# Loading w of the first four chunks in two-token runs of 320 bytes, with running sums by pair member

## The chip, the cores and the metric

The kernel runs on one core of a Trainium2 chip. The core has a matrix engine (PE, with its weight loads shown as PEld), a vector engine (DVE), an activation engine (ACT), a general engine (POOL), a queue engine (SP) and 16 DMA engines that move data between the chip's memory (HBM) and the on-chip buffers. Each engine takes its instructions in order. The metric is the device time of one execution in microseconds (us).

## The reference

A recurrent attention over 768 tokens, for 4 batches of 8 heads of 40 features each (`r`, `k`, `v`, `w`, `a`, `b`, each 4 x 8 x 768 x 40, float32), and then a feed-forward layer on the result:

```python
for t in range(S):
    y[:, :, t] = np.einsum('bhd,bhde->bhe', rt, state)
    Sa = np.einsum('bhde,bhe->bhd', state, at)
    state_decay = state * wt[:, :, None, :] - np.einsum('bhd,bhe->bhde', Sa, bt)
    state = state_decay + np.einsum('bhd,bhe->bhde', vt, kt)
...
h = x @ w_in
g = np.maximum(h, 0.0) ** 2
return g @ w_out
```

Here `x` is `y` laid out as 3072 tokens of 320 features; `w_in` is 320 x 2048, `w_out` 2048 x 320. `w` decays the state at each token, so over a stretch of tokens it enters as a product, which the kernel forms as the exponential of a running sum of logarithms.

## The kernel before

The tokens are cut into 12 chunks of 64. Tokens of a chunk lie on partitions: 64 for the batches 0 and 1 (g = 0) and 64 for the batches 2 and 3 (g = 1). A batch of such a group is called here a member, and each member has 8 heads. So `raw_w`, 128 x 16 x 40 numbers, has on partition 64g + t the 16 heads of group g at token t.

For each chunk c the kernel does this with w:

- `ldw c` loads it (`load`, `go_w`), in two transfers of 160 KB, each with runs of 40 numbers, 160 bytes. For chunk 0 there are four transfers of 80 KB, by group and member: member 0 (`ldw 0 h0`) on SP, member 1 (`ldw 0 h1`) on ACT.
- `ln c` (ACT, L598) takes the logarithm into `lnW`; `hi c` and `lo c` split it into two bf16 parts (`hi` a cast, `lo` the rest). For chunk 0 each is done in two halves, by member.
- `ci c` and `cf c` (PE, recorded at L388) form the running sums over the chunk's tokens by multiplying with a triangle of ones. `ci` puts tokens on partitions (320 columns a matmul), `cf` puts features on partitions and tokens on columns. For chunks 0 to 3 `ci` uses the 128 x 128 matrix `UTB`, two triangles of 64 on the diagonal, so one matmul covers both groups. `cf` of chunks 0, 1 and 2 uses `UTB` too (`wide_sums`); `cf` of chunk 3 and of all later chunks works in pairs of 64-row matmuls with `UTI`, one for each group.
- `ec`, `eg` and `ef` (ACT, L624, L562, L674) are exponentials of the sums, into `Gin`, `iG` and `GT`. `eg` of chunk 0 is done in two halves.
- `tb`, `tk` (DVE, L580) and `tA` (DVE, L712) multiply turned k, b and a with `iG` and `GT`; what follows are the triangles `EN` and `CX` (DVE, L737), the state `S`, `s` (L838), and the feed-forward matmuls (L958 and L388).

For chunks 0 to 3 (`BY8`) k, b, a and r are loaded in runs of eight tokens, 1280 bytes, and turned by PE; v is loaded in 160-byte runs in all chunks. From chunk 4 on k and b are loaded in 160-byte runs too.

The order of the work on each engine is written out by hand in `ORDER`, and the program issues exactly that order. The loads on SP begin: `ldw 0 h0`, `ldb 0`, `ldk 0`, `lda 0`, `ldw 1`, `ldv 0`, `ldb 1`, `ldr 0`, `ldw 2`, `lda 2`, `ldv 1`, `ldw 3`, `ldb 2`, `ldk 2`, `ldv 2`, `ldr 1`. On PE `TR 0` (r of chunk 0 turned) stands ahead of `NU 0`, `TA 1` and `TU 1`.

The constants (`UTI`, `UTB`, `IDQ`, `IDb`, `MSK`, `MSKI`) are made at the start by POOL's `affine_select`, 14 instructions of 64 x 64 (L266); the casts of w of chunk 0 on POOL stand behind them.

## Time and profile before

| | |
|---|---|
| time, three runs | 237.29, 237.42, 239.2 us; median 237.42 |
| the profiled execution, its own time | 238.79 us |
| its span, from the first to the last instruction | 237.1 us |
| mean granted TensorE clock | 0.998 |
| packets of all DMA queues | 121689 of 38.78 MB, 105770 of them under 512 bytes |
| transfers of w on SP | 22 of 160 KB and 2 of 80 KB; 2 more of 80 KB on ACT |

A page of the profile shows the busy time of each engine, the chain of work that ended last (followed back from the last instruction, at each step to what released it), groups of instructions by line, and the DMA queues. Other views show the chain in order of time, the instructions of an engine in order of time, and the busy time in given stretches. Times count from the start of the span. A DMA that SP issues shows as SPq with the time that the issue took; the transfer lands later. In brackets stands how long an engine was idle before an instruction, and what released it. "x2" merges two instructions that follow one another.

### The profile page before, as it was taken

To read this page: it belongs to the slowest core of one execution; us is meant where nothing else is said; L and a number is where in the kernel's file an instruction comes from. 1 tells how busy PE (TensorE), PEld (TensorE's weight loads), DVE (VectorE), ACT (ScalarE), POOL (GpSimd) and SP (SyncE) were. 2 spreads that over 40 slices of the span, in tenths; PEclk is the share of its full clock that TensorE was granted. 3 is DMA by queue.
4 is the path that set the end of the run, shared out by engine and by line. 5 is a ranking of instruction groups with operands and counts; after the bars stand their busy time and mean duration, and the time that the engine had idled before them with its cause. 6 is when DMAs were issued, how large, how long until landed. Compare 5 with 4: busy or idle time off the path is not lost.

```text
span 237.1 us, 11681 instructions
## 1 busy us (share of the span) xinstructions
PE 217.9 (92%) x5249; PEld 167.7 (71%) x5249; DVE 181.0 (76%) x236; ACT 175.0 (74%) x233; POOL 130.9 (55%) x138
## 2 busy tenths in 40 slices
PE   7587887889999999999998999999987999999993
PEld 2366776668787777777776778777775777877771
DVE  7468999697989877888977989799877687756220
ACT  3637957848997996897997989996767984652911
POOL 8552729056696547579394944907986620730600
PEclk9999999999999999999999999999999999999999
DMA  5998879998898998999999889989998995931104
GB/s 122 209 228 154 176 160 260 271 210 203 269 179 165 174 191 155 157 187 156 181 166 188 173 151 170 177 179 184 177 155 165 186 159 124 194 13 30 30 3 110
DMA packets 121689, 38.78 MB, mean 164 GB/s; under 512 B 105770, under 2 KB 121638, under 8 KB 121638
## 3 DMA queue, kind: packets, MB, share of 16 engines
q1 hardware_dynamic: 119862, 37.04, 82.4%
q10 hardware_dynamic: 1776, 0.98, 1.6%
q8 instruction: 41, 0.67, 1.2%
q14 instruction: 10, 0.08, 0.1%
HBM read 28.84 MB, written 3.93 MB: 138 GB/s over the span
## 4 chain that ended last, share of the span: by engine, by line
PE 74%; DMA 7%; SPq 7%; ACT 3%; issue 3%; DVE 2%; POOL 2%; ACTq 0%; POOLq 0%; DVEq 0%
PE pb L388 43%; PE pb L958 23%; PE pb L392 5%; PE pb L396 3%; DMA KBT<-KB 3%; DMA raw_r<-in_r_dram 2%; DMA raw_kb<-in_b_dram 2%; SPq L445 2%; SPq L430 2%; SPq L454 2%; ACT VU L374 1%; DVE STb L838 1%; ACT GT L674 1%; SPq L432 1%; POOL lo L382 1%
## 5 line engine op out<-in xcount | busy, mean ns | idle before, releaser
L994 POOL TENSOR_TENSOR G<-G 128x1024 bf16<-128x1024 bf16 x22 | 41.6, 1896 | 35.9 <-ACT G L986 33.8
L388 PE MATMUL pb<-WOUT,G 128*128 128x320 bf16 x384 | 56.9, 300 | 0.0
L958 PE MATMUL pb<-XT,WIN 128*128 128x256 bf16 x384 | 48.7, 273 | 1.1 <-ACT VU L374 1.0
L986 ACT ACTIVATE G<-pb 128x1024 bf16<-128x1024 f32 x39 | 39.3, 1021 | 12.1 <-PE pb L958 10.2
L388 PEld LDWEIGHTS <-G 128*128 128x128 bf16 x384 | 35.6, 98 | 14.1 <-issue 0.2
L958 PEld LDWEIGHTS <-WIN 128*128 128x128 bf16 x384 | 34.8, 98 | 8.5 <-issue 2.4
L737 DVE TENSOR_TENSOR CX<-pb,MSKI 128x1024 bf16<-128x1024 f32 x24 | 28.9, 1221 | 5.8 <-PE pb L388 5.6
L737 DVE TENSOR_TENSOR EN<-pb,MSK 128x1024 bf16<-128x1024 f32 x24 | 29.0, 1217 | 4.3 <-PE pb L388 3.8
L382 POOL TENSOR_TENSOR KB<-raw_kb,iG 128x640 bf16<-128x640 f32 x12 | 18.4, 1543 | 5.5 <-DMA raw_a<-in_a_dram 2.9
L712 DVE TENSOR_TENSOR AR<-pb,GT 128x512 bf16<-128x512 bf16 x24 | 15.8, 685 | 4.6 <-PE pb L396 1.8
L838 DVE TENSOR_TENSOR STb<-pb,GT 40x640 bf16<-40x640 f32 x22 | 18.1, 821 | 0.6
L996 ACT ACTIVATE G<-G 128x1024 bf16<-128x1024 bf16 x17 | 17.8, 1053 | 0.2
L382 POOL TENSOR_TENSOR lo<-lnW,hi 128x640 bf16<-128x640 f32 (+1 forms) x10 | 13.5, 1352 | 7.4 <-ACT hi L374 6.2
L958 PE MATMUL pb<-XT,WLAST 64*128 64x256 bf16 x192 | 17.5, 272 | 0.0
L388 PEld LDWEIGHTS <-EN 64*64 64x64 bf16 (+1 forms) x768 | 14.6, 110 | 3.2 <-issue 2.5
L378 POOL CAST hi<-lnW 128x640 bf16<-128x640 f32 (+1 forms) x10 | 6.9, 692 | 16.7 <-ACT lnW L598 15.9
L374 ACT ACTIVATE osb<-pb 128x640 f32<-128x640 f32 (+1 forms) x10 | 6.5, 650 | 12.2 <-PE pb L388 12.1
L647 ACT ACTIVATE Gin<-pb 64x320 f32<-64x320 f32 x32 | 13.7, 429 | 2.0 <-PE pb L388 1.5
L920 DVE TENSOR_TENSOR Yb<-pb,Gin 128x640 bf16<-128x640 f32 (+1 forms) x24 | 12.4, 551 | 3.2 <-PE pb L388 3.1
L374 ACT ACTIVATE VU<-pb 64x640 bf16<-64x640 f32 x17 | 11.8, 696 | 3.8 <-PE pb L388 3.5
L374 ACT ACTIVATE AR<-pb 128x512 bf16<-128x512 bf16 x20 | 11.0, 596 | 4.7 <-PE pb L392 3.5
L988 DVE TENSOR_SCALAR G<-pb 128x1024 bf16<-128x1024 f32 x9 | 11.0, 1223 | 3.5 <-PE pb L958 3.3
(131 smaller groups left out, 442.8 us busy)
## 6 DMA issues: line engine op xcount, KB each, us to landing
raw_kb<-in_b_dram SPq DMA_DIRECT2D x24, 160.0 KB, 4.3
raw_v<-in_v_dram SPq DMA_DIRECT2D x24, 160.0 KB, 4.4
raw_kb<-in_k_dram SPq DMA_DIRECT2D x22, 160.0 KB, 5.0
raw_a<-in_a_dram SPq DMA_DIRECT2D x22, 160.0 KB, 4.9
raw_w<-in_w_dram SPq DMA_DIRECT2D x22, 160.0 KB, 4.4
raw_r<-in_r_dram SPq DMA_DIRECT2D x22, 160.0 KB, 4.1
out_dram<-osb SPq DMA_DIRECT2D x22, 160.0 KB, 2.6
G<-in_moe_w_in_dram SPq DMA_DIRECT2D x10, 256.0 KB, 5.8
```

Of the source, the lines that this page charges most:

```text
L374: alts.append(("ACT", c_act(n), lambda: nc.scalar.activation(out=o_(), in_=i_(), func=ACTF.Copy, scale=1.0 if scale is None else scale)))
L382: return [("POOL", 40 + 2.35 * n, lambda: nc.gpsimd.tensor_tensor(out=o_(), in0=a_(), in1=b_(), op=op)), ("DVE", c_dve(n), lambda: nc.vect ...
L388: return lambda: nc.tensor.matmul(out=o_(), lhsT=l_(), rhs=r_(), start=start, stop=stop, skip_group_check=True)
L647: nc.scalar.activation(out=Gin[c % NGI][rows(g), NP * jh:NP * jh + NP, :].rearrange("p j e -> p (j e)"), in_=slot(hb, FP32)[rows(g), g, 0: ...
L712: ew(f"tA {c} g{g}", [("DVE", c_dve(512), lambda g=g: nc.vector.tensor_tensor(out=steps(AR[q2][:, 0, g]), in0=turned(ha, g), in1=steps(GT[ ...
L737: ew(f"m{nm} {c} g{g}", [("DVE", c_dve(1024), lambda: nc.vector.tensor_tensor(out=dst[q2][:, g].rearrange("p q i t -> p (q i) t"), in0=slo ...
L838: ew(f"s {c} q{q}", [("DVE", c_dve(2 * n), lambda q=q: nc.vector.tensor_tensor(out=STb[q2][live(q), :, q, 0:D], in0=slot(hs, FP32)[live(q) ...
L920: return [("DVE", c_dve(2 * (f1 - f0)), lambda: nc.vector.tensor_tensor(out=Yb[q2][:, :, to:to + f1 - f0], in0=slot(hy, FP32)[:, :, f0:f1] ...
L958: return lambda: nc.tensor.matmul(out=o_(), lhsT=l_(), rhs=r_(), start=begins and opens(hf, x), stop=ends and not opens(hf, x), skip_group ...
L986: ("ACT", c_act(1024), lambda gb=gb, hf=hf: nc.scalar.activation(out=gb, in_=slot(hf, FP32)[:], func=ACTF.Relu)),
L994: ("POOL", 1900, lambda gv=gv: nc.gpsimd.tensor_tensor(out=gv, in0=gv, in1=gv, op=ALU.mult)),
L996: ("ACT", c_act(1024), lambda gv=gv: nc.scalar.activation(out=gv, in_=gv, func=ACTF.Square))],
```

## The change

For chunks 0 to 3 w is loaded with two consecutive tokens in one run of 80 numbers, 320 bytes. A pair of tokens now lies on one partition: partition 64x + 32g + p holds tokens 2p and 2p + 1 of member x of group g, with 8 heads of two tokens. That takes four transfers of 80 KB a chunk, by member and group. Chunk 0 has as many as before, two on SP and two on ACT; chunks 1, 2 and 3 have four on SP.

The logarithm writes `lnW` with the token of the pair (i) outermost, 8 heads each. A running sum is then over pairs and over the two members of a pair: for each member x of the batches (its 64 partitions), for each i, and for `hi` and `lo`, one 64-row matmul with the matrix `UT2[rows(x), i]`, 64 x 128, which puts the tokens of both groups into 128 columns. `ci` of a chunk becomes eight 64-row matmuls of 320 columns (chunk 0: two times eight of 160) for four of 128 rows; `cf` becomes 32 64-row matmuls of 128 columns, for 16 of 128 rows (chunks 0, 1, 2) or 32 64-row ones of 64 columns (chunk 3). The sums come out in the places that they had in chunks 0 to 2.

The halves of chunk 0 are now by heads (0 to 3, 4 to 7 of each member), so both halves of `ln 0` read all four transfers, and each half of `eg 0` is two instructions. `UTB` is gone; `UT2` is made by four `affine_select` of 64 x 128 from a mask that DVE writes into `EN` beforehand with three memsets, and `UTI` by two of 64 x 128 for four of 64 x 64. `ORDER` is as it was.

```diff
-    UTB = buf("UTB", [128, 128], BF16)[0]
...
+    UT2 = buf("UT2", [128, 2, 128], BF16)[0]
...
+    gate = EN[0][:].rearrange("p a b c d -> p (a b c d)")[:, 0:128]
+    nc.vector.memset(gate, 1.0)
+    for g in range(2):
+        nc.vector.memset(gate[64 * g:64 * g + 32, 64:128], 0.0)
+    for g in range(2):
+        for i in range(2):
+            nc.gpsimd.affine_select(out=UT2[rows(g), i, :], in_=gate[rows(g), :],
+                                    pattern=[[1, 128]], compare_op=ALU.is_ge, fill=0.0,
+                                    base=-i, channel_multiplier=-2)
...
+        nc.gpsimd.affine_select(out=UTI[rows(g), :].rearrange("p (x t) -> p x t", x=2),
+                                in_=ones[rows(g), :].rearrange("p (x t) -> p x t", x=2),
+                                pattern=[[0, 2], [1, 64]], compare_op=ALU.is_ge, fill=0.0,
+                                base=0, channel_multiplier=-1)
...
         def go_w(js, q_):
-            for g in range(2):
-                if len(js) == 2:
-                    q_.dma_start(out=raw_w[c % NW][rows(g)], in_=half(w, g))
-                else:
+            for x in js if c in BY8 else ():
+                for g in range(2):
+                    p0 = 64 * x + 32 * g
                     q_.dma_start(
-                        out=raw_w[c % NW][rows(g), NP * js[0]:NP * js[0] + NP, :],
-                        in_=w[2 * g + js[0], :, t0, :].rearrange("h t e -> t h e"))
+                        out=raw_w[c % NW][p0:p0 + 32].rearrange("p (h i) e -> p h (i e)", i=2),
+                        in_=w[2 * g + x, :, t0, :].rearrange("h (p i) e -> p h (i e)", i=2))
+            for g in range(0 if c in BY8 else 2):
+                q_.dma_start(out=raw_w[c % NW][rows(g)], in_=half(w, g))
...
-        return c == 0 or f"cf {c}" in WHOLE
...
-        if wide_sums(c):
+        if c in BY8:
             return flat(h, FP32).rearrange("p (m g t) -> p g m t", g=2, t=L)
...
+                for at in ([slice(4 * y + 2 * js[0], 4 * y + 2 * js[0] + 2) for y in range(2)]
+                           if len(js) == 1 else [slice(0, 8)]):
+                    nc.scalar.activation(out=o_[:, :, at], in_=i_[:, :, at], func=ACTF.Exp,
+                                         scale=-1.0)
...
-               reads=[("raw", "w", c % NW, jh) for jh in js] + [("act",)],
+               reads=[("raw", "w", c % NW, jh) for jh in range(2)] + [("act",)],
...
+                for x in (h_, l_):
+                    for i in range(2):
+                        for g in range(2):
+                            ms.append(mm(
+                                lambda g=g, a0=a0, a1=a1: slot(hd, FP32)[:, g, 0:n].rearrange(
+                                    "p (j e) -> p j e", e=D)[:, a0:a1],
+                                lambda g=g, i=i: UT2[rows(g), i, :],
+                                lambda x=x, g=g, i=i, a0=a0, a1=a1: x[
+                                    rows(g), 8 * i + a0:8 * i + a1, 0:D],
+                                x is h_ and i == 0 and a0 == 0, x is l_ and i == 1))
...
+            for p in range(2 * js[0], 2 * js[-1] + 2) if c in BY8 else ():
                 for x in (h_, l_):
-                    if wide_sums(c):
-                        ms.append(mm(
-                            lambda p=p: flat(hf, FP32)[:, 128 * p:128 * p + 128],
...
+                    for i in range(2):
+                        for g in range(2):
+                            ms.append(mm(
+                                lambda p=p, g=g: slot(hf, FP32)[:, g, 128 * p:128 * p + 128],
+                                lambda x=x, p=p, g=g, i=i: x[
+                                    rows(g), 8 * i + 2 * p:8 * i + 2 * p + 2, :].rearrange(
+                                        "p h e -> p (h e)"),
+                                lambda g=g, i=i: UT2[rows(g), i, :],
+                                x is h_ and i == 0 and p == 0, x is l_ and i == 1))
```

More of the change, by code (lines that the diff above doesn't have):

```diff
@@ L267, in tri_const @@
                                 base=0, channel_multiplier=-1)
-    UTB = buf("UTB", [128, 128], BF16)[0]
-    IDQ = buf("IDQ", [128, 128], BF16)[0]
-    nc.vector.memset(UTB[:], 0.0)
-    nc.vector.memset(IDQ[:], 0.0)
-    for g in range(2):
-        for x in range(2):
-            tri_const(UTI[rows(g), rows(x)], ones[rows(g), 0:64], ALU.is_ge)
-    for g in range(2):
-        tri_const(UTB[rows(g), rows(g)], ones[rows(g), 0:64], ALU.is_ge)
-    for g in range(2):
-        tri_const(IDQ[rows(g), rows(g)], ones[rows(g), 0:64], ALU.is_equal)
-    for g in range(2):
-        tri_const(IDb[rows(g), :], ones[rows(g), 0:64], ALU.is_equal)
-    for g in range(2):
-        tri_const(MSK[rows(g), :], ones[rows(g), 0:64], ALU.is_gt)
-    for g in range(2):
-        tri_const(MSKI[rows(g), :], ones[rows(g), 0:64], ALU.is_ge)
     NW, NKBR, NA, NR, NV = 2, 2, 2, 2, 2
@@ L322 @@
     WOUT = buf("WOUT", [128, NFB, DM], BF16)[0]
+    UT2 = buf("UT2", [128, 2, 128], BF16)[0]
+    IDQ = buf("IDQ", [128, 128], BF16)[0]
+    gate = EN[0][:].rearrange("p a b c d -> p (a b c d)")[:, 0:128]
[7 more added lines that the diff above has]
+                                    base=-i, channel_multiplier=-2)
+    nc.vector.memset(IDQ[:], 0.0)
+    for g in range(2):
[4 more added lines that the diff above has]
+    for g in range(2):
+        tri_const(IDQ[rows(g), rows(g)], ones[rows(g), 0:64], ALU.is_equal)
+    for g in range(2):
+        tri_const(IDb[rows(g), :], ones[rows(g), 0:64], ALU.is_equal)
+    for g in range(2):
+        tri_const(MSK[rows(g), :], ones[rows(g), 0:64], ALU.is_gt)
+    for g in range(2):
+        tri_const(MSKI[rows(g), :], ones[rows(g), 0:64], ALU.is_ge)
     for x in GT:
@@ L427, in go_w @@
         def go_w(js, q_):
-            for g in range(2):
-                if len(js) == 2:
-                    q_.dma_start(out=raw_w[c % NW][rows(g)], in_=half(w, g))
-                else:
+            for x in js if c in BY8 else ():
+                for g in range(2):
+                    p0 = 64 * x + 32 * g
                     q_.dma_start(
-                        out=raw_w[c % NW][rows(g), NP * js[0]:NP * js[0] + NP, :],
-                        in_=w[2 * g + js[0], :, t0, :].rearrange("h t e -> t h e"))
+                        out=raw_w[c % NW][p0:p0 + 32].rearrange("p (h i) e -> p h (i e)", i=2),
+                        in_=w[2 * g + x, :, t0, :].rearrange("h (p i) e -> p h (i e)", i=2))
+            for g in range(0 if c in BY8 else 2):
+                q_.dma_start(out=raw_w[c % NW][rows(g)], in_=half(w, g))
         for js in ((0,), (1,)) if c == 0 else ((0, 1),):
@@ L511, in flat @@
         return slot(h, dt)[:].rearrange("p b x -> p (b x)")
-    def wide_sums(c):
-        return c == 0 or f"cf {c}" in WHOLE
     def sums(c, h):
-        if wide_sums(c):
+        if c in BY8:
             return flat(h, FP32).rearrange("p (m g t) -> p g m t", g=2, t=L)
@@ L559, in keys_by8, with exps @@
         for js in ((0,), (1,)) if c == 0 else ((0, 1),):
-            at = slice(4 * js[0], 4 * js[-1] + 4)
-            ew(f"eg {c}" + f" h{js[0]}" * (2 - len(js)), [
-                ("ACT", c_act(512 * len(js)), lambda at=at: nc.scalar.activation(
-                    out=igt.rearrange("p (g m) t -> p g m t", g=2)[:, :, at],
-                    in_=sums(c, hf)[:, :, at], func=ACTF.Exp, scale=-1.0))],
+            def exps(js=js):
+                o_ = igt.rearrange("p (g m) t -> p g m t", g=2)
+                i_ = sums(c, hf)
+                for at in ([slice(4 * y + 2 * js[0], 4 * y + 2 * js[0] + 2) for y in range(2)]
+                           if len(js) == 1 else [slice(0, 8)]):
+                    nc.scalar.activation(out=o_[:, :, at], in_=i_[:, :, at], func=ACTF.Exp,
+                                         scale=-1.0)
+            ew(f"eg {c}" + f" h{js[0]}" * (2 - len(js)), [("ACT", c_act(512 * len(js)), exps)],
                reads=[hf + (jh,) for jh in js], writes=[("iG", jh) for jh in js], free=[hf])
@@ L596, in prep, with part, log @@
         for js in ((0,), (1,)) if c == 0 else ((0, 1),):
-            x, at, k_ = f" h{js[0]}" * (2 - len(js)), slice(NP * js[0], NP * js[-1] + NP), 320 * len(js)
-            ew(f"ln {c}{x}", [("ACT", c_act(k_), lambda at=at: nc.scalar.activation(
-                out=lw[:, at], in_=raw_w[c % NW][:, at], func=ACTF.Ln))],
-               reads=[("raw", "w", c % NW, jh) for jh in js] + [("act",)],
+            x, k_ = f" h{js[0]}" * (2 - len(js)), 320 * len(js)
+            def part(t, js=js):
+                if len(js) == 2:
+                    return t
+                return t.rearrange("p (i h) e -> p i h e", i=2)[:, :, 4 * js[0]:4 * js[0] + 4]
+            def log(js=js, part=part):
+                o_, i_ = lw[:], raw_w[c % NW][:]
+                if c in BY8:
+                    o_ = o_.rearrange("p (i h) e -> p i h e", i=2)
+                    i_ = i_.rearrange("p (h i) e -> p i h e", i=2)
+                    at = slice(4 * js[0], 4 * js[-1] + 4)
+                    o_, i_ = o_[:, :, at], i_[:, :, at]
+                nc.scalar.activation(out=o_, in_=i_, func=ACTF.Ln)
+            ew(f"ln {c}{x}", [("ACT", c_act(k_), log)],
+               reads=[("raw", "w", c % NW, jh) for jh in range(2)] + [("act",)],
                writes=[("lnW", jh) for jh in js])
-            ew(f"hi {c}{x}", copy_alts(lambda at=at: h_[:, at, 0:D], lambda at=at: lw[:, at], k_,
+            ew(f"hi {c}{x}", copy_alts(lambda part=part: part(h_[:, :, 0:D]),
+                                       lambda part=part: part(lw[:]), k_,
                                        True, engines=("POOL", "DVE", "ACT")),
                reads=[("lnW", jh) for jh in js], writes=[("hi", jh) for jh in js])
-            ew(f"lo {c}{x}", mul_alts(lambda at=at: l_[:, at, 0:D], lambda at=at: lw[:, at],
-                                      lambda at=at: h_[:, at, 0:D], k_, ALU.subtract),
+            ew(f"lo {c}{x}", mul_alts(lambda part=part: part(l_[:, :, 0:D]),
+                                      lambda part=part: part(lw[:]),
+                                      lambda part=part: part(h_[:, :, 0:D]), k_, ALU.subtract),
                reads=[("lnW", jh) for jh in js] + [("hi", jh) for jh in js],
@@ L613, in prep @@
                 ms = []
-                for jh in js:
-                    for x in (h_, l_):
-                        ms.append(mm(
-                            lambda jh=jh: slot(hd, FP32)[:, jh, 0:n].rearrange(
-                                "p (j e) -> p j e", e=D),
-                            lambda: UTB[:], lambda x=x, jh=jh: x[:, NP * jh:NP * jh + NP, 0:D],
-                            x is h_, x is l_))
-                pe(f"ci {c}" + f" h{js[0]}" * (2 - len(js)), "D", n, ms,
+                a0, a1 = 4 * js[0], 4 * js[-1] + 4
+                for x in (h_, l_):
+                    for i in range(2):
+                        for g in range(2):
+                            ms.append(mm(
[5 more added lines that the diff above has]
+                                x is h_ and i == 0 and a0 == 0, x is l_ and i == 1))
+                pe(f"ci {c}" + f" h{js[0]}" * (2 - len(js)), "R", 160 * len(js), ms,
                    reads=[(x, jh) for x in ("hi", "lo") for jh in js], writes=[hd],
@@ L654, in prep @@
             ms = []
-            for p in range(4 * js[0], 4 * js[-1] + 4):
+            for p in range(2 * js[0], 2 * js[-1] + 2) if c in BY8 else ():
                 for x in (h_, l_):
-                    if wide_sums(c):
-                        ms.append(mm(
-                            lambda p=p: flat(hf, FP32)[:, 128 * p:128 * p + 128],
-                            lambda x=x, p=p: x[:, 2 * p:2 * p + 2, :].rearrange(
-                                "p h e -> p (h e)"),
-                            lambda: UTB[:], x is h_ and p % 4 == 0, x is l_))
-                        continue
+                    for i in range(2):
+                        for g in range(2):
+                            ms.append(mm(
[5 more added lines that the diff above has]
+                                x is h_ and i == 0 and p == 0, x is l_ and i == 1))
+            for p in range(0 if c in BY8 else 8):
+                for x in (h_, l_):
                     for g in range(2):
@@ L670, in prep @@
             pe(f"cf {c}" + f" h{js[0]}" * (2 - len(js)),
-               *(("D", 128) if wide_sums(c) else ("R", L)), ms,
+               "R", 128 if c in BY8 else L, ms,
                reads=[(x, jh) for x in ("hi", "lo") for jh in js],
```

## The prediction

> **What bounds the kernel now.** I read the page first, then the windows, then the chain of waits in order of time, then the timelines of SP and DVE over the first 36 us. From the page:

> ```profile
> span 237.1 us, 11681 instructions
> PE 217.9 (92%) x5249; PEld 167.7 (71%) x5249; DVE 181.0 (76%) x236; ACT 175.0 (74%) x233; POOL 130.9 (55%) x138
> q1 hardware_dynamic: 119862, 37.04, 82.4%
> PE 74%; DMA 7%; SPq 7%; ACT 3%; issue 3%; DVE 2%; POOL 2%; ACTq 0%; POOLq 0%; DVEq 0%
> ```

> PE is busy 92% of the span and holds 74% of the chain. DMA and the SP queue hold 14%, and the question is where. The windows (length, then busy time and instructions of PE, PEld, DVE, ACT, POOL, clock, DMA share, GB/s) and four rows of the chain (start, duration, what) answer it:

> ```profile
> 0.00:20.00 20.00, 14.71 (x187) 9.21 (x187) 13.83 (x35) 9.87 (x14) 11.45 (x28) 1.00 0.89 180
> 20.00:36.00 16.00, 13.06 (x426) 11.26 (x423) 14.43 (x19) 12.80 (x16) 7.69 (x11) 1.00 0.78 170
> 60.00:100.00 40.00, 39.63 (x1000) 30.68 (x994) 32.93 (x40) 34.40 (x48) 25.45 (x25) 1.00 0.91 185
> ```

> ```profile
> 13.95 5.90 DMA raw_r<-in_r_dram
> ...
> 25.80 5.34 DMA raw_kb<-in_b_dram
> ...
> 39.23 0.76 PE pb L388 x40
> ...
> 45.63 1.05 PE pb L958 x8
> ```

> From 60 us on PE works 39.63 of 40 us: nothing about loads of w can speed that up, but a time won earlier passes through it to the end. In the first 36 us PE has 8.2 us of idle (36 less 14.71 and 13.06), and the chain goes through loads: r of chunk 0 lands 5.90 us after its issue, b of chunk 2 after 5.34. That is the only stage where the change acts, since it concerns w of chunks 0 to 3.

> **The SP queue.** SP issues nearly all loads in one fixed order. Its timeline (start, duration, transfers; nothing between them but a few tenths):

> ```profile
> 5.16 1.24 SPq L460 DMA_DIRECT2D raw_a<-in_a_dram  x2
> 6.44 1.60 SPq L430 DMA_DIRECT2D raw_w<-in_w_dram  x2
> 8.09 3.64 SPq L454 DMA_DIRECT2D raw_v<-in_v_dram  x2
> 14.67 1.36 SPq L430 DMA_DIRECT2D raw_w<-in_w_dram  x2
> 16.12 4.31 SPq L460 DMA_DIRECT2D raw_a<-in_a_dram  x2
> 21.91 3.02 SPq L430 DMA_DIRECT2D raw_w<-in_w_dram  x2
> 24.97 1.43 SPq L445 DMA_DIRECT2D raw_kb<-in_b_dram  x2
> ```

> An undisturbed pair takes 1.24 (a, 5.16) to 1.36 us (w, 14.67): 0.62 to 0.68 us an issue. Three pairs take much longer: v of chunk 0 by 2.4, a of chunk 2 by 3.07, w of chunk 3 by 1.66 us, 7.1 us together. Each stands behind, or is, a load in 160-byte runs. I read these as a queue that is full until packets ahead have been served.

> **Price of a packet.** Two windows of one microsecond, one while w of chunk 1 and v of chunk 0 (160-byte runs) are under way, one while b and r (1280-byte runs) are:

> ```profile
> 12.00:13.00 1.00, 1.00 (x12) 0.61 (x10) 0.43 (x1) 0.00 (x0) 0.00 (x0) 1.00 1.11 169
> 15.00:16.00 1.00, 0.37 (x5) 0.23 (x6) 1.00 (x2) 0.67 (x1) 1.00 (x1) 1.00 0.98 284
> ```

> At a share of one these are 169/1.11 = 152 and 284/0.98 = 290 GB/s, so with 16 engines a 160-byte packet takes 16 x 160/152 = 16.8 ns and a 1280-byte packet 70.6 ns. The line through both gives 24.5 ns for 320 bytes, which no row shows. The bounds are 16.8 (a packet costs the same whatever its size) and 33.6 ns (cost goes by bytes). A chunk's w is 2048 packets now and 1024 after, so its service goes from 2.15 us to 1.57: **0.58 us saved a chunk**, bounds 1.08 and 0. I take 0.58, since the 1280-byte row, eight times the bytes for four times the time, rules out both ends.

> [...]

> **Issues.** Chunk 0 keeps two transfers on SP and two on ACT. Chunks 1, 2 and 3 have four on SP for two: six more issues at about 0.65 us, 3.9 us more work on SP by b of chunk 2. Everything behind w in SP's order is moved past: v, b, r of chunks 0 and 1, a and b of chunk 2. I cost it at nothing because the 7.1 us of stalls cover it: an issue that is made later finds the queue emptier. Without that cover it costs 3.9 us (rival one).

> **First chunk.** Rows of the timeline, with the idle time in brackets, then groups by shape:

> ```profile
> 5.30 0.83 ACT L598 ACTIVATE lnW<-raw_w 128x320 f32<-128x320 f32 x2 [1.75 <-DMA raw_w<-in_w_dram]
> 5.87 0.52 POOL L266 TENSOR_SCALAR_AFFINE_SELECT MSKI<-ones 64x64 bf16<-64x64 bf16 x2
> 6.46 0.45 POOL L378 CAST hi<-lnW 128x320 bf16<-128x320 f32 x1
> 13.38 0.74 ACT L598 ACTIVATE lnW<-raw_w 128x640 f32<-128x640 f32 x1 [2.05 <-DMA raw_w<-in_w_dram]
> ```

> ```profile
> L378 POOL CAST KB<-raw_kb 128x640 bf16<-128x640 f32 x6 | 4.3, 718 | 3.3 <-DMA raw_kb<-in_b_dram 3.1
> L562 ACT ACTIVATE iG<-pb 128x1024 f32<-128x1024 f32 x3 | 3.1, 1026 | 1.4 <-PE pb L388 1.4
> L562 ACT ACTIVATE iG<-pb 128x512 f32<-128x512 f32 x2 | 1.2, 597 | 1.5 <-PE pb L388 1.4
> L266 POOL TENSOR_SCALAR_AFFINE_SELECT UTI<-ones 64x64 bf16<-64x64 bf16 x4 | 0.8, 236 | 0.1
> ```

> Both logarithms of chunk 0 now wait for both halves of w. Before they ran back to back from 5.30, so the halves landed together and the wait adds nothing. But an earlier landing helps little: POOL's constants end at 6.39 (5.87 + 0.52) and the cast of the second half follows at 6.46. There are 14 selects before and after, six of them now 128 columns wide. By POOL's casts (718 ns for 640 columns, 450 for 320: 0.84 ns a column) the 64 added columns cost 54 ns each, 0.32 us in all; bounds 0 (one price) and 1.4 us (6 x 236 ns, price by columns). I take 0.32. The three small memsets added on DVE go before POOL is free of its first memset, and cost nothing. The exponential of chunk 0 is cut from two halves into four quarters: by 597 and 1026 ns, 0.84 ns an element, a quarter is 0.38 us, so each half grows by 0.17, 0.33 in all on ACT, in parallel to POOL's delay. So DVE's first product moves from 9.94 to about 10.3. DVE's timeline shows the cover:

> ```profile
> 9.94 1.89 DVE L580 TENSOR_TENSOR KBT<-pb,iG 128x512 bf16<-128x512 bf16 x3 [2.69 <-PE pb L396]
> 12.57 0.69 DVE L712 TENSOR_TENSOR AR<-pb,GT 128x512 bf16<-128x512 bf16 x1 [0.74 <-PE pb L396]
> 14.93 0.83 DVE L384 TENSOR_TENSOR lo<-lnW,hi 128x640 bf16<-128x640 f32 x1 [1.08 <-POOL hi L378]
> 22.58 1.29 DVE L712 TENSOR_TENSOR AR<-pb,GT 128x512 bf16<-128x512 bf16 x2 [0.83 <-PE pb L396]
> 32.69 1.29 DVE L580 TENSOR_TENSOR KBT<-pb,iG 128x512 bf16<-128x512 bf16 x2 [0.38 <-PE pb L396]
> ```

> Three products, then 0.74 us idle before 12.57, where a of chunk 0 is late. The 0.33 us fits into that: nothing on the path; if the cover fails, +0.33.

> **Matmuls.** Every full 128-row matmul becomes a pair of 64-row ones, one on each half of the rows. Rows of the running sums of chunk 1 (full, 128 columns) and chunk 3 (already in pairs, 64 columns), first and last of each run:

> ```profile
> 15.88 0.22 PE L388 MATMUL pb<-UTB,hi 128*128 128x128 bf16 x1
> 16.61 0.22 PE L388 MATMUL pb<-UTB,lo 128*128 128x128 bf16 x1
> 39.23 0.21 PE L388 MATMUL pb<-UTI,hi 64*128 64x64 bf16 x2
> 39.66 0.21 PE L388 MATMUL pb<-UTI,lo 64*128 64x64 bf16 x2
> ```

> Fourteen full matmuls start over 0.73 us, 56 ns apart; in chunk 3 sixteen pairs start over 0.43 us, 29 ns a pair. So pairs overlap, and a pair of 128 columns should take about 57 ns, as the full one did: nothing for chunks 0 to 2 and for the sums by token (four full of 320 columns become four pairs). Without overlap each would double; the chunk 3 rows speak against it. Chunk 3's 16 pairs double their columns: 16 x 28 ns = **+0.45 us**, in the chain at 39.23. The logarithms, casts and exponentials of chunks 1 to 3 keep their element counts.

> **The sum.** Three of DVE's idles give way. (1) Before 14.93: the logarithm of chunk 1 waited 2.05 us for w and began at 13.38. Half the packets of w0 and w1 put 2 x 0.58 = 1.16 us less ahead of its landing, and its last issue moves from 8.04 to about 9.0, well ahead of that: about -1.0, the idle of 1.08. (2) Before 22.58: the transposes of chunk 1 stand on PE behind r of chunk 0, which lands at 19.85 (13.95 + 5.90). The same 1.16 us come off it, so the shift grows only to -1.2. (3) Before 32.69: b of chunk 2 gets all four savings, 2.3 us, more than the shift there; its 0.38 us idle goes: -1.6. Chunk 3's pairs give back 0.45: -1.15, say **-1.2 us**, bounds +0.45 (no packet saving) and -2.5 (1.08 a chunk, 2.2 at (2) and 0.38 at (3), and chunk 3's pairs hidden). After that PE carries it to the end. Profiled, the execution took 238.79 us, 1.7 more than its span; by that it would be 237.6. The median of the three runs is 237.42 (237.29 to 239.2), and I set the shift against it: **236.2 us**, own range 234.9 to 237.9.

> **Rivals.** *SP becomes the bound* (slower): the stalls count transfers, not packets, and do not shrink. The six issues then push b of chunk 2 back by their 3.9 us, and DVE already waits for it at 32.69; with chunk 3's 0.45 that is 241.8 us. For it: the windows 20 to 36 show DMA at a share of 0.78, so it isn't packets alone that hold SP. Against it: the pair of a at 5.16, with only 1280-byte runs of b and k just ahead, doesn't stall. The kernel gets slower where the stalls shrink by less than 4.35 of their 7.1 us (3.9 + 0.45), and by over 1% below about 2; the forecast needs some 6. [...] *Nothing reaches the end*: DVE, 14.43 of 16 us busy in the second window, and the longer first chunk swallow it: 237.4. *More than forecast*: the loads come so early that DVE's idles of 0.74, 1.08, 0.83 and 0.38 us all go and chunk 3's pairs hide: 3.0 us, 234.4; for it the 290 GB/s of long runs, against it POOL's constants.

> **How the numbers follow.** Forecast 0.43, more 0.17, nothing (with stalls that shrink halfway) 0.16, SP 0.24. Under 1% (2.4 us) a measurement of this kernel hardly differs from no change. Faster by more: 0.17 and 0.03 of the forecast's edge. Slower by more: 0.24, the SP rival. Within: 0.56. The range, 234.2 to 240.3, leaves out the outer part of the SP rival (about 0.13) and of the large gain (0.06).

> **What would show it.** Right: the packets of queue q1 fall by 4096 from 119862; the pair of v of chunk 0 and of a of chunk 2 take under 2.5 us on SP though they start later; the logarithm of chunk 1 starts by about 12.4, b of chunk 2 lands before 30 us; pairs of 64-row sums start 56 ns apart. Wrong: stalls of the same length behind more issues; the selects at 0.4 us or more and DVE's first product after 10.5; 64-row matmuls that start one after the other; a new wait on DMA after 45 us that eats the shift.

## The result, and the profile after

| | before | after |
|---|---|---|
| time, median of 20 runs each | 237.98 us | 240.4 us |
| span of the profiled execution | 237.1 us | 236.9 us |
| ratio after to before | | 1.0129, 95% interval 1.0093 to 1.0165 |

The kernel got slower, by 1.3% [0.9%, 1.7%], where 236.2 us and a small gain were forecast. The ratio is taken over those runs that lie within 1.5% of the fastest of their kernel, while the medians in the table are of all runs. The two spans nearly agree, and that is the first thing to learn here: one record is one execution. The profiled run of before took 238.79 us, above its median, and that of after 238.6 us, near the low end of its runs (238.1 to 244.48).

The page of after: instructions, PE, the two DMA queues that matter below (packets, MB, share of 16 engines), and the chain's shares.

```profile
span 236.9 us, 11838 instructions
PE 219.0 (92%) x5321; PEld 169.1 (71%) x5321; DVE 181.5 (77%) x238; ACT 174.8 (74%) x235; POOL 132.0 (56%) x138
q1 hardware_dynamic: 116374, 37.04, 78.1%
q8 instruction: 41, 0.67, 1.2%
PE 77%; DVE 8%; issue 5%; ACT 4%; SPq 3%; DMA 1%; POOL 1%; ACTq 0%; POOLq 0%
```

The packets fell as forecast: 3488 fewer on q1 (of the 4096, 512 show on q10, which went from 1776 to 1264, and q1 has 96 more packets of 4 bytes, 16 for each of the six more transfers). DMA and SPq are down from 14% to 4% of the chain, and DVE is up from 2% to 8%. PE has 72 matmuls and 72 weight loads more, 144 instructions. And "issue", time in which an engine waits for nothing that the profile shows, went from 3% to 5%. SP's timeline of after (start, duration, transfers) answers to the stalls shown of before:

```profile
5.64 2.10 SPq L438 DMA_DIRECT2D raw_w<-in_w_dram  x4
9.05 1.43 SPq L462 DMA_DIRECT2D raw_v<-in_v_dram  x2
...
13.35 4.47 SPq L438 DMA_DIRECT2D raw_w<-in_w_dram  x4
17.92 1.18 SPq L468 DMA_DIRECT2D raw_a<-in_a_dram  x2
...
20.58 3.32 SPq L438 DMA_DIRECT2D raw_w<-in_w_dram  x4
23.95 2.26 SPq L453 DMA_DIRECT2D raw_kb<-in_b_dram  x2
```

The pair of v went from 3.64 to 1.43 us, the pair of a from 4.31 to 1.18. But most of SP's waiting only moved. It now stands still for 1.31 us ahead of v (7.74 to 9.05), the four transfers of w take 4.47 and 3.32 us where the first four took 2.10, and the pair of b takes 2.26 where the one at 10.52 took 1.31. Together that is 5.9 us of stalls for the 7.1 of before, and SP is done with b of chunk 2 at 26.21 us for 26.40.

Then the waits of PE for "issue", by line (us in total, times, longest), of before and of after:

```profile
PE pb L392 <- issue: 2.4, 3, 1.0
PE pb L388 <- issue: 1.3, 4, 0.5
```

```profile
PE pb L395 <- issue: 3.7, 6, 0.9
PE pb L989 <- issue: 1.0, 1, 1.0
PE pb L399 <- issue: 0.9, 1, 0.9
PE pb L403 <- issue: 0.6, 1, 0.6
```

3.7 us have become 6.2. Where they stand, PE's timeline shows (start, duration, operation, tiles, count, idle before it): once in after, in the middle of 32 equal matmuls, and once among 16 equal transposes.

```profile
84.69 0.56 PE L395 MATMUL pb<-VU,EN 128*64 128x40 bf16 x24
85.70 0.30 PE L395 MATMUL pb<-VU,EN 128*64 128x40 bf16 x8 [0.45 <-issue]
...
123.01 0.28 PE L399 MATMUL pb<-IDb,tR 64*128 64x64 bf16 x8
124.21 0.29 PE L399 MATMUL pb<-IDb,tR 64*128 64x64 bf16 x8 [0.92 <-issue]
```

### The profile page after: what moved, and what is told of

The parts are those of the page before. It is cut to its first block, busy times and chain, and to the rows that moved or that the text cites. A ratio compares the mean times of both kernels' runs of the same rounds, so it can differ in the third digit from the quotient of the medians.

```text
span 236.9 us, 11838 instructions
## 1 busy us (share of the span) xinstructions
PE 219.0 (92%) x5321; PEld 169.1 (71%) x5321; DVE 181.5 (77%) x238; ACT 174.8 (74%) x235; POOL 132.0 (56%) x138
## 3 DMA queue, kind: packets, MB, share of 16 engines
q1 hardware_dynamic: 116374, 37.04, 78.1%
q10 hardware_dynamic: 1264, 0.98, 1.4%
## 4 chain that ended last, share of the span: by engine, by line
PE 77%; DVE 8%; issue 5%; ACT 4%; SPq 3%; DMA 1%; POOL 1%; ACTq 0%; POOLq 0%
PE pb L395 44%; PE pb L989 24%; PE pb L399 6%; PE pb L403 3%; DVE EN L768 2%; DVE KBT L588 2%; DVE AR L743 2%; ACT G L1017 1%; DMA raw_w<-in_w_dram 1%; DVE STb L869 1%; SPq L453 1%; SPq L438 1%; DVE CX L768 1%; ACT Gin L674 1%; POOL lo L389 1%
## 5 line engine op out<-in xcount | busy, mean ns | idle before, releaser
L395 PEld LDWEIGHTS <-G 128*128 128x128 bf16 x384 | 35.8, 98 | 13.9 <-POOL G L1025 0.2
L389 POOL TENSOR_TENSOR lo<-lnW,hi 128x640 bf16<-128x640 f32 (+1 forms) x10 | 13.4, 1339 | 10.3 <-ACT hi L381 6.2
L951 DVE TENSOR_TENSOR Yb<-pb,Gin 128x640 bf16<-128x640 f32 (+1 forms) x24 | 12.4, 552 | 3.7 <-PE pb L395 3.2
L588 DVE TENSOR_TENSOR KBT<-pb,iG 128x512 bf16<-128x512 bf16 x16 | 10.2, 682 | 4.8 <-ACT iG L570 4.0
```

Of the source, the lines that this page charges most:

```text
L389: return [("POOL", 40 + 2.35 * n, lambda: nc.gpsimd.tensor_tensor(out=o_(), in0=a_(), in1=b_(), op=op)), ("DVE", c_dve(n), lambda: nc.vect ...
L395: return lambda: nc.tensor.matmul(out=o_(), lhsT=l_(), rhs=r_(), start=start, stop=stop, skip_group_check=True)
L588: nc.vector.tensor_tensor(out=steps(KBT[q2][:, NP * g:NP * g + NP, g if x else 1 - g]), in0=turned(h, g), in1=steps(igt[:, NP * g:NP * g + ...
```

## The experiments

"Before" and "after" name the two kernels; each run was timed beside the kernel before on one chip, whose medians were 237.08 to 238.67 us.

**After, once more.** Unchanged, to see whether the result holds: the lines of PE's waits repeat.

> The changed kernel once more, for a second trace and its time beside the variants. Theory one (instruction blocks): the matrix engine's code arrives in blocks of 256 instructions, its waits without a releaser stand only at block boundaries (matmul records 256 apart), and the 144 instructions that the change adds on that engine move the boundaries into dense stretches; then the ratio is again 1.01 to 1.017 and the new trace has its waits at the same block positions, summing to 5 to 7 us against 3.7 in the kernel before. Theory two (SP): the six extra issues and the earlier loads disturb the transfers after 36 us; then the same ratio, but the waits have releasers (DMA, or engines fed by it).

239.41 us, ratio 1.0093 [1.0052, 1.0133]. "Issue" takes 6.5 us of PE. The slowdown is about 1%.

**Empty instructions in the warm-up.** Three kernels pad PE's program with empty instructions between the 14 warm-up matmuls: before with 144, after with 112 (144 + 112 = 256: boundaries as in before, a block later), before with 256 as control.

```diff
-        for _ in range(n):
+        for m in range(n):
             nc.tensor.matmul(...)
+            for _ in range(144 * (m + 1) // n - 144 * m // n):
+                nc.tensor.nop("pad", nofuse=True)
```

> The kernel before with 144 empty instructions on the matrix engine among its warm-up matmuls, where they cost nothing that follows waits for: code positions as in the changed kernel from chunk 4 on, loads as before. Theory one: slower than before by 1 to 2% (239.5 to 242 us), since the loss comes without the early gain of 1.7 us. Theory two: within 0.3% of before.

> The changed kernel with 112 empty instructions at the same place: 144 + 112 = 256, so from chunk 4 on every boundary stands where it stood before the change, one block later. Theory one: faster than before by 0.4 to 0.8% (236 to 237 us), the early gain kept. Theory two: as slow as the changed kernel, ratio 1.01 to 1.017.

> The kernel before with 256 empty instructions at the same place: a whole block, boundaries where they were. A control for the empty instructions themselves. Theory one and theory two: within 0.4% of before. If it is slower by 1% or more, the number of instructions and not their position costs, and theory one needs another form.

Ratios 1.0296 [1.0236, 1.0355], 1.0133 [1.0086, 1.018] and 1.0548 [1.0488, 1.0608]. The control failed: both theories expected nothing of it. The empty instructions were not free; they stretched the warm-up and moved DVE's first product to 15.4 and 24.8 us (from 9.94 in before) and to 13.9 us (from 11.01 in after). Inconclusive as times.

**Pairs of small matmuls instead.** The same counts, now as pairs of 64-row matmuls, four instructions a pair with the weight loads, in the gap that PE has between the last warm-up matmul and the first sum. Nothing reads their result.

```diff
         warm(14)
+        for _ in range(36):
+            for h in range(2):
+                nc.tensor.matmul(out=banks[0][:, h, 0:64], lhsT=ones[rows(h), :],
+                                 rhs=ones[rows(h), 0:64], start=True, stop=True,
+                                 skip_group_check=True)
         plan.issue(ORDER)
```

> The kernel before, with 144 more instructions on TensorE behind the warm-up: 36 pairs of matmuls of 64 rows and 64 columns over ones, whose result nothing reads. They fall into the gap of over 1 us between the last warm-up matmul and the first running sum, and at about 30 ns a pair take about 1 us of it. Nothing else is changed; the boundaries of TensorE's 256-instruction blocks stand from here on where they stand in the kernel after. Theory one (blocks): the time rises by 1 to 4 us (ratio 1.005 to 1.017), with the steps of the loss where the kernel after lost: between 69 and 76 us, 85 and 92 us, 118 and 128 us. Theory two (SP and its transfers): no change, ratio 0.997 to 1.003.

> The kernel after, with 112 more instructions on TensorE in the same gap (28 pairs of the same small matmuls). 144 + 112 = 256: the block boundaries stand where they stand in the kernel before, one block later. Theory one (blocks): the losses at 69 to 76, 85 to 92 and 118 to 128 us are gone, and what the earlier w brought is kept: ratio 0.992 to 1.000, well below that of the kernel after. Theory two: the time of the kernel after, ratio 1.007 to 1.015.

> A control: the kernel before with a whole block of 256 instructions on TensorE in that gap (64 pairs, about 1.9 us, so up to 0.7 us past the moment at which the first running sum could start). The boundaries stand at the same instructions as before. Both theories: ratio 0.998 to 1.005. If it is above 1.007, the small matmuls themselves cost time and the other two runs must be read with that taken off.

Ratios: 1.0173 [1.0097, 1.025] for before with 144; 0.9946 [0.9878, 1.0014] for after with 112; 1.0005 [0.9919, 1.0091] for the control. These agree with theory one: instructions that do nothing slow before down when they move the boundaries, not when they move them by a whole block. The 1.0173 lies just above the range expected, and of the three stretches named for the loss, 69 to 76 us has no such wait with 144. The same place in PE's timeline, of after with 112 pairs and then of before with 144:

```profile
82.56 0.69 PE L395 MATMUL pb<-VU,EN 128*64 128x40 bf16 x32
...
120.47 0.40 PE L399 MATMUL pb<-IDb,tR 64*128 64x64 bf16 x16
```

```profile
126.15 0.28 PE L392 MATMUL pb<-IDb,tR 64*128 64x64 bf16 x8
128.45 0.29 PE L392 MATMUL pb<-IDb,tR 64*128 64x64 bf16 x8 [2.02 <-issue]
```

With 112 instructions ahead of after, the row of 32 and the row of 16 run through; with 144 ahead of before, the row of 16 breaks where it broke in after, for 2.02 us. The page of after with 112 has one block more:

```profile
q8 instruction: 42, 0.69, 1.2%
```

**Four transfers of the old runs.** Before, with w of chunks 1 to 3 in four transfers of 160-byte runs: SP's six more issues alone.

```diff
-                if len(js) == 2:
+                if len(js) == 2 and c not in BY8:
                     q_.dma_start(out=raw_w[c % NW][rows(g)], in_=half(w, g))
-                else:
+                    continue
+                for x in js:
                     q_.dma_start(
-                        out=raw_w[c % NW][rows(g), NP * js[0]:NP * js[0] + NP, :],
-                        in_=w[2 * g + js[0], :, t0, :].rearrange("h t e -> t h e"))
+                        out=raw_w[c % NW][rows(g), NP * x:NP * x + NP, :],
+                        in_=w[2 * g + x, :, t0, :].rearrange("h t e -> t h e"))
```

> The kernel before with w of chunks 1 to 3 loaded in four transfers a chunk, of the 160-byte runs that it has (64 tokens of one pair member each), in place of two: SP's six more issues without the longer packets, and with no change on TensorE. Theory two (the six issues and what they push back): the time rises by 1.5 to 3 us, ratio 1.006 to 1.013. Theory one: 0.997 to 1.004, since SP's stalls of 7.1 us cover 3.9 us of issues and the blocks stand as before.

Ratio 0.9999 [0.9955, 1.0042]. The issues cost nothing that this interval can show (1 us), and the second theory falls, as does the prediction's slower rival.

**Can the cost be counted beforehand?** Two more places, 64 instructions (16 pairs) ahead of after and 80 (20 pairs) ahead of before, with a forecast from the length of each stretch of 256 instructions.

> The kernel after with 64 more instructions on TensorE (16 pairs of the small matmuls) in the gap behind the warm-up: a third place of the block boundaries. In the trace of after each stretch of 256 instructions is timed with its stalls taken out, and whatever a stretch falls short of 3.8 us (or 4.1 us: the packet of the next block has been seen to start 1 to 2.5 us after a boundary, to take about 1 us, and TensorE to go on about 1.4 us after it) is counted as a stall. With the boundaries of after that gives 4.5 us (7.3 us), with 64 instructions ahead of them 3.0 us (5.3 us), with 112 0.8 us (2.5 us). Theory one (blocks): 1.5 to 2.0 us below after and about 2.5 us above the run with 112, so a ratio to before of 1.001 to 1.007. Theory three (what helped was matmuls in the gap, not the place of the boundaries): the ratio of the run with 112 instructions, 0.99 to 1.00.

> The kernel before with 80 more instructions on TensorE (20 pairs) in that gap. The same count on the trace of before gives stalls of 0.4 us (1.9 us at 4.1 us a block) with its own boundaries, 2.2 us (4.9 us) with 80 instructions ahead and 5.4 us (8.1 us) with 144. Theory one (blocks): 1.8 to 3.0 us slower than before, ratio 1.006 to 1.013, between before and the run with 144. Theory three (only the place 144 hurts, or the number of small matmuls counts): the ratio of the control with 256, 0.995 to 1.005.

Ratios 1.0107 [1.0039, 1.0175] and 1.0014 [0.9963, 1.0065]. The first lies above the figure expected, though its interval holds part of it; the second below, and nearer to no change. So the place matters, but this count doesn't give the time.

**After with 112, again and a third time.**

> The kernel after with 112 instructions in the gap, as it ran before, to see whether it is faster than the kernel before: at that place of the boundaries the trace of after counts 0.8 us of block stalls, against 0.4 us for before, so what is left of the change is the gain that the prediction worked out, 1.2 us less the difference: ratio 0.994 to 0.999.

> The kernel after with 112 instructions in the gap, without the move, a third time: 0.995 to 1.003 (0.9946 and 1.0034 so far), the fifth group of k and b products at 31.16 us where the clock is full.

Ratios 1.0034 [1.0002, 1.0067] and 1.0127 [1.0054, 1.0201], after 0.9946 the first time. Both lie above what was expected, and three comparisons of one kernel differ by more than their intervals allow; their plain mean is 1.0036. By the medians of all runs the three ratios are 1.0004, 1.0035 and 1.0081, which lie closer together and have the mean 1.004. In the third record "issue" takes 4.0 us, in the first two 1.7 and 1.8: equal boundaries don't make equal waits. And there the fifth group of k and b products started at 32.24 us, not 31.16, with the clock at 1.00. The two runs of after have 1.0129 and 1.0093, mean 1.0111.

**The new transfers alone, and before unchanged.** Before with w of chunks 1 to 3 loaded as in after, the old sums over it; its sums run over the tokens in another order, so it computes something else. And before itself, three more records.

```diff
-            for g in range(2):
+            for x in js if c in (1, 2, 3) else ():
+                for g in range(2):
+                    p0 = 64 * x + 32 * g
+                    q_.dma_start(
+                        out=raw_w[c % NW][p0:p0 + 32].rearrange("p (h i) e -> p h (i e)", i=2),
+                        in_=w[2 * g + x, :, t0, :].rearrange("h (p i) e -> p h (i e)", i=2))
+            for g in range(0 if c in (1, 2, 3) else 2):
```

> The kernel before, with w of chunks 1 to 3 loaded as the change loads it (two-token runs of 320 bytes, four transfers a chunk) and everything else as it was: the sums then run over tokens in another order, so this kernel computes something else. TensorE's instructions stand as in before. If the longer packets bring w earlier (the prediction: 1.0 us at chunk 1, 1.2 us at chunk 2, 1.6 us at chunk 3), the logarithms of chunks 2 and 3 start about 1 to 1.5 us ahead of those of the unchanged records, and the ratio is 0.993 to 0.998. If loading is not what sets the pace there, they start where the unchanged records have them within 0.3 us, and the ratio is 0.998 to 1.003.

> The kernel before, unchanged: how far two equal kernels differ. Ratio 0.997 to 1.003. If the profiled run of before was slow in its loading stage by chance, the logarithm of chunk 3 starts here at 31.5 to 32.5 us with the clock at 1.00 up to there; if it was ordinary, at 33.5 to 34 us.

> The kernel before, unchanged: another record of the same stage, with the same two cases (31.5 to 32.5 us by chance slow before, 33.5 to 34 us ordinary).

> The kernel before, unchanged: a third further record of the same stage, with the same two cases.

Ratios 1.0002 [0.9947, 1.0057] for the transfers and 1.0002 [0.995, 1.0053] for before against itself; the single times of the two further records were 240.01 and 237.42 us. The logarithms of chunks 1, 2 and 3 start at:

```
before, profiled first    13.38  22.97  33.84
before, three records     13.27  22.16  32.55 | 12.74  22.62  33.43 | 12.48  21.52  31.56
new transfers alone       12.11  21.52  31.55
after, both records       12.38  21.88  32.13 | 12.39  21.89  32.15
after with 112, three     12.38  21.88  32.13 | 12.39  21.90  33.78 | 13.28  22.16  33.30
```

In each of the three columns the record from which the prediction was made is the latest of all. The unchanged kernel scatters over 0.9, 1.45 and 2.3 us there, and after lies inside that scatter at chunks 2 and 3. With 112 instructions ahead, after scatters as well, by 0.9 and 1.65 us at chunks 1 and 3 (at 30 to 36 us the clock was 0.72 in its second record, 1.00 in the others).

**DVE's clearing moved.** After with 112 instructions, and the clearing of STb (0.91 us) behind DVE's `lo` of the first half, twice.

```diff
-ORDER = """DVE zs 1; SP ldw 0 h0; ...
+ORDER = """SP ldw 0 h0; ...
...
-... DVE lo 0 h0; PE1 cf 0 h0; ...
+... DVE lo 0 h0; DVE zs 1; PE1 cf 0 h0; ...
```

> The kernel after with 112 instructions in the gap, and DVE's clearing of STb (0.91 us) moved behind DVE's lo of the first half in the written order. In after that clearing and the lo ran at 5.7 to 7.0 us beside a pair of POOL selects that took 1.70 us in place of 0.52 us. If the two engines hold each other up there, the pair falls to 0.5 to 0.7 us, POOL's hi starts 0.9 to 1.2 us earlier and the first product of DVE 0.4 to 0.9 us earlier. The end: no change against the run without the move (within 0.3 us, ratio 0.993 to 1.000), since from 14 us on the second w sets the pace and it lands when it did.

> The kernel after with 112 instructions in the gap and DVE's clearing of STb behind the lo of the first half, as it ran before. If DVE's own work from its first product on sets the pace to 36 us, the fifth group of k and b products starts at 30.2 us where the clock is full (31.16 without the move), and the time is 0.5 to 1.0 us below the run without the move (its ratio lower by 0.002 to 0.004, ratio to before 0.994 to 0.999). If something later takes it back, the ratios of the two runs are equal within 0.002.

Ratios 1.0061 [1.0012, 1.0111] and 1.0024 [0.9949, 1.0099], mean 1.004, against 1.0036 without the move: no gain at the end that these runs can tell. In both records the clock fell to between 0.72 and 0.77 at 30 to 36 us, so the stage behind can't be read. What stood beside POOL's selects, in before, in after and with the move (its first run):

```profile
5.31 0.52 POOL L266 TENSOR_SCALAR_AFFINE_SELECT MSK<-ones 64x64 bf16<-64x64 bf16 x2
5.34 0.91 DVE L1095 MEMSET STb<- 128x1024 uint32 x1 [0.26 <-issue]
```

```profile
5.67 1.70 POOL L266 TENSOR_SCALAR_AFFINE_SELECT MSK<-ones 64x64 bf16<-64x64 bf16 x2
5.73 0.91 DVE L1126 MEMSET STb<- 128x1024 uint32 x1 [0.26 <-issue]
6.56 0.43 DVE L391 TENSOR_TENSOR lo<-lnW,hi 128x320 bf16<-128x320 f32 x1
7.99 0.45 POOL L385 CAST hi<-lnW 128x320 bf16<-128x320 f32 x1
```

```profile
5.51 0.49 DVE L391 TENSOR_TENSOR lo<-lnW,hi 128x320 bf16<-128x320 f32 x1
5.69 0.69 POOL L266 TENSOR_SCALAR_AFFINE_SELECT MSK<-ones 64x64 bf16<-64x64 bf16 x2
6.17 0.91 DVE L1126 MEMSET STb<- 128x1024 uint32 x1 [0.16 <-issue]
6.43 0.52 POOL L266 TENSOR_SCALAR_AFFINE_SELECT MSKI<-ones 64x64 bf16<-64x64 bf16 x2
7.02 0.45 POOL L385 CAST hi<-lnW 128x320 bf16<-128x320 f32 x1
10.06 1.97 DVE L588 TENSOR_TENSOR KBT<-pb,iG 128x512 bf16<-128x512 bf16 x3 [2.98 <-ACT iG L570]
```

The pair of selects fell from 1.70 to 0.69 us, POOL's `hi` came 0.97 us earlier, and DVE's first product at 10.06 in place of 11.01 (0.4 to 0.9 us earlier were expected). In the second run it came at 10.89, so that last step isn't firm. Nor is it the clearing alone that holds the selects up: in before, and with the move, selects ran beside it at 0.52 us a pair. What was held is one select, and it ended behind DVE's subtraction `lo`: in after it took 1.41 us, to 7.08, where `lo` ended at 6.99; with the move 0.41 us, to 6.10, where `lo` ended at 6.00. Why in after it was held from the clearing on, when `lo` stood right behind that, no run shows.

## Why the prediction was wrong

**The step that failed is "After that PE carries it to the end", with the matmuls costed by array time alone.** "So pairs overlap, and a pair of 128 columns should take about 57 ns, as the full one did: nothing for chunks 0 to 2" was right for the array: the pairs start 57 ns apart in after. But a pair is four instructions for two, and the 144 more moved the boundaries of all later blocks. The sums of PE's waits for "issue", one figure a record:

```
boundaries of before   before 3.7, 3.0, 5.8, 0.9; four transfers 3.4; new transfers 2.5; 256 pairs' control 2.5
                       after with 112: 1.7, 1.8, 4.0; with the clearing moved 2.8, 2.7
boundaries of after    after 6.2, 6.5; before with 144: 8.0
other places           after with 64: 6.8; before with 80: 4.6
```

(The 8.0 and the 6.8 are of records with a mean clock of 0.979 and 0.986.) At the boundaries of before the middle value is 2.75 us, at those of after 6.5: some 3.7 us more waiting, for 2.2 to 3.1 us more time (0.93% and 1.29% of 237.98). That the waits come from the place was shown from both sides: 144 idle instructions cost before 1.7%, and 112 ahead of after bring its mean ratio from 1.0111 to 1.0036. How much of the 1.1% that is stays open: by the mean two thirds, by the single runs anything from none to all.

What a wait hangs on, the records say too. In 17 of them (all but those with empty instructions) PE waited for "issue" 108 times, over 0.15 us each, and all 108 stand on one grid of 256 instructions. On it 658 boundaries between 12 and 215 us can be placed. Where PE needed over 5 us for the block before, it then paused for over 0.4 us at 1 of 265; where it needed 4 to 5 us, at 33 of 263; where it needed under 4 us, at 76 of 130. At such a pause PE goes on 1.2 to 1.8 us after the block's packet has landed (108 of 110; 2.5 us at most), and that packet starts only 2.1 us (middle value) after the boundary before. In after, at the broken row of 16:

```
boundary before it   packet of the next block    row breaks   goes on
119.93               121.53 to 122.63            123.10       124.21
```

From one boundary to going on behind the next passed 4.28 us: 1.60 until the packet starts, 1.10 for the packet, 1.58 behind it. The stretch itself took 3.17 us; the other 1.11 is the gap. So the time until the next block is there was nearly always hidden behind the slow stretches (1 pause at 265 boundaries) and mostly not behind the dense ones (76 at 130).

**The forecast gain: the baseline.** "About -1.0" before 14.93, "-1.2" before 22.58 and "-1.6" before 32.69 were taken against one record, and against it the changed kernel did gain 1.53 us at 32.69 (31.16). Against the first of the further records of before, with a span of 233.8 us, the same rows of DVE read:

```profile
9.96 1.89 DVE L580 TENSOR_TENSOR KBT<-pb,iG 128x512 bf16<-128x512 bf16 x3 [2.69 <-PE pb L396]
12.17 0.69 DVE L712 TENSOR_TENSOR AR<-pb,GT 128x512 bf16<-128x512 bf16 x1 [0.32 <-PE pb L396]
14.83 0.83 DVE L384 TENSOR_TENSOR lo<-lnW,hi 128x640 bf16<-128x640 f32 x1 [1.37 <-POOL hi L378]
22.05 1.29 DVE L712 TENSOR_TENSOR AR<-pb,GT 128x512 bf16<-128x512 bf16 x2 [0.41 <-PE pb L396]
31.60 1.28 DVE L580 TENSOR_TENSOR KBT<-pb,iG 128x512 bf16<-128x512 bf16 x2
```

Two of the three idles that were to give way are small or gone here: 0.41 us for 0.83, none for 0.38. The same rows in after:

```profile
11.01 1.99 DVE L588 TENSOR_TENSOR KBT<-pb,iG 128x512 bf16<-128x512 bf16 x3 [4.02 <-ACT iG L570]
14.26 1.12 DVE L391 TENSOR_TENSOR lo<-lnW,hi 128x640 bf16<-128x640 f32 x1
21.77 1.29 DVE L743 TENSOR_TENSOR AR<-pb,GT 128x512 bf16<-128x512 bf16 x2 [0.41 <-PE pb L403]
31.16 1.28 DVE L588 TENSOR_TENSOR KBT<-pb,iG 128x512 bf16<-128x512 bf16 x2
```

The idles of 0.32 and 1.37 us did go, since w of chunk 1 is there in time. But from 11.01 on DVE works with hardly a break (19.64 us busy of the 20.16 to 31.16), so it sets the pace of this stage, and its start is 1.05 us later: 0.44 us are left at 31, and chunk 3's wider pairs (+0.45 forecast) use that up. The two other records of before have the fifth group at 32.29 and 30.77 us, so against them after is 1.13 us earlier and 0.39 us later. So without the blocks one would expect a shift near nothing, not -1.2, but with a scatter as large as the forecast; the new transfers alone (1.0002) don't contradict that, though at an interval of half a per cent they can't show 0.4 us either.

**The first chunk** was mis-sized. "So DVE's first product moves from 9.94 to about 10.3", and "The 0.33 us fits into that: nothing on the path": it came at 11.01. The wider selects cost what was forecast (UT2's four took 1.14 us); the rest is the one 64-column select that took 1.41 us and ended 0.09 us behind DVE's subtraction. And the cover of 0.74 us was another property of the one record: in the next three it was 0.32, 0.15 and 0.15 us.

**The issues: right at the end, not on the way.** "I cost it at nothing because the 7.1 us of stalls cover it" held at the end, but the stalls did not shrink by the 6 us that the forecast needed: they fell by 1.2, to 5.9. By the prediction's own rule, under about 2 means over 1% slower. That the kernel did become 1% slower is chance: the issues alone cost nothing (0.9999), so that rule, too, was wrong.

**Right** were the fewer packets and, to the letter, v and a under 2.5 us on SP. Right, too, but no proof of a gain, were the logarithm of chunk 1 at 12.38 ("by about 12.4"), since the unchanged kernel has 12.48 in one record, and b of chunk 2 before 30 us: issued at 24.55, it landed 3.8 us later, and in two of the three further records of before it landed before 30 us as well.

No version beat before: after with 112 instructions, with or without the move, has mean ratios of 1.004.

## What to carry to other kernels

Here 144 more instructions on the engine that sets the pace moved every later boundary of its blocks of 256, and 144 that did nothing cost before 1.7%, where the change was to bring 0.5%: count the instructions, look in the trace for pauses without a releaser in the middle of equal work, and test with a pad that moves the boundaries back, beside a control of a whole block. Before idles of under a microsecond are counted on, take a second record of the unchanged kernel: here they moved by as much as the forecast gain. And a pad must be measured with nothing else changed; 256 empty instructions cost 5.5% (1.0548).

## What the runs showed of the hardware

- An empty PE instruction had a cost: 256 of them in the warm-up moved ACT's first exponential of a running sum from 7.91 to 21.50 us (13.59 us, 53 ns each) and DVE's first product from 9.94 to 24.77 us, while 256 instructions as 64 pairs of matmuls in the gap moved that product by 1.0 us, to 10.94.
- A select of 64 x 64 on POOL took 0.23 to 0.24 us in before, also beside DVE's clearing of 128 x 1024 words (the pair at 5.31). In after, where DVE's subtraction `lo` stood right behind that clearing, one took 1.41 us, and ended 0.09 us behind `lo`; with `lo` ahead of the clearing one took 0.41 us, and ended 0.10 us behind `lo`. What holds a select up, no run shows.
- Four transfers of 80 KB in 320-byte runs took 2.10 us of SP's issue time (0.52 each) at 5.64 us in after, against 1.60 us for two of 160 KB in before.
